# Batch 0 keys sorted for four destinations first, batch 1 values sorted later, column sums on TensorE, and zeros ahead of small products

## The chip, the cores and the metric

One core of a Trainium2 chip. Times are device microseconds (us) of whole executions; profiles are single executions, timed by the hardware profiler from first to last instruction (about 2 us less than the time of a run). The kernel before took 242.44 us (median of 4).

Engines: PE is TensorE (matrix products), PEld its weight loads, DVE VectorE, ACT ScalarE, POOL GpSimd, SP the engine that issues most small DMAs. L12 is line 12 of that run's kernel; line numbers shift by 2 to 28 between the two kernels.

## The reference, cut to what matters

```python
for _ in range(5):                      # P: 4 x 8 matrices of 8 x 8 (Sinkhorn)
    P = exp(P - max(P)); P = P / sum over columns; P = P / sum over rows
k_sorted = einsum('bhij,bhjcd->bhicd', P, k_blocks)      # 8 blocks of 96 tokens
v_sorted = einsum('bhij,bhjcd->bhicd', P, v_blocks)
attn     = softmax(q_block @ k_sorted_block.T / 8) @ v_sorted_block
x = attn as (3072 tokens, 512)
h = x @ w_in                            # 512 -> 2048
out = (s * relu(h)**2 + b) @ w_out      # 2048 -> 512
```

The kernel works on eight tiles of 384 tokens, two per batch. `ffn1(t)` is the first product (its PSUM tile is `hps`) and `ffn2(t)` the second (`ops`). As b is a constant, b times the column sums of w_out is added as a bias.

## The kernel before

All large loads go through one queue, that of POOL, in program order. The values of batches 0 and 2 share the lower half of one tile, those of 1 and 3 the upper half:

```python
vb = const.tile([128, 128, D], BF)
def load_v(rows, prow):
    nc.gpsimd.dma_start(out=vb[prow, 0:BLK, :], in_=vraw[rows])
```

The values of batch 1 are sorted in six pieces (`V1`), written to DRAM and read back in another layout (tile `vs`), as attention needs them with tokens on the partitions:

```python
def v_piece1(c0, eng):                  # two products, one copy, two DMAs to DRAM
    for hf in range(2):
        nc.tensor.matmul(out=ps[hf*64:(hf+1)*64], lhsT=lhsT, rhs=vb[pr, ...], ...)
    evac(vn[:, 0:8, :], ps, eng)
    for hf in range(2): nc.sync.dma_start(out=dv[1][...], in_=vn[...])
```

The schedule around it (cuts marked ...):

```python
warm_up(38); q_half(0, "s"); warm_up(12); build_pd1()
k_piece(0, 0, 16, 1, "v")() ...         # keys of batch 0, all eight destinations
v_piece0(...), s_piece(0, ...) ...      # values and scores of tile 0
q_half(1, "s"); p_piece(0, hp, 0, 2) x4; t_piece(0, "v", 0, 2); s_piece(1, 0); s_piece(1, 1)
load_v(*brows(2))
ffn1(0, Queue([P(0,0,2,2) ... SC(1,3), P(1,0)], 8), 0, 2)
ffn1(0, Queue([V1(0), P(1,1), V1(1), P(1,2), V1(2), P(1,3), V1(3), t_piece(1)], 8), 2, 2)
V1(4)(); V1(5)()
csums(0, 8)                             # on POOL, half of the column sums
v_read(1, nc.sync)                      # values of batch 1 back from DRAM
ffn1(1, Queue([nothing]*4 + [build_pd2] + [nothing]*3, 8))
load_v(*brows(3))
csums(8, NF)                            # on POOL, the other half
# slots of ffn2(0), ffn2(1): q and k pieces of batch 1, then load_k(2), load_k(3), load_q(2),
# S2(2,0) ... P2(2,0) ...               P2(2,0) is the first that needs the values read back
```

`S2` is two score pieces, `P2` two pieces of weighted values, `T` a transposition by DMA. A `Queue` puts its pieces between the products, one per slot.

The softmax here doesn't subtract the row's maximum and nothing guards it: scores larger than these inputs give would overflow.

Of the kernel before, what the change touches and what calls it, by code (L numbers as in the profile page):

```python
# [9 lines left out]
FP = mybir.dt.float32  # L10
# [8 lines left out]
def kernel(  # L19
# [126 lines left out]
            out=w, in_=moe_w_in.rearrange("(hp p) f -> p hp f", p=128)[:, :, c0:c0 + FCH])  # L146
        wis.append(w)
    onesf = const.tile([128, 128], FP)
    nc.gpsimd.memset(onesf, 1.0)

    load_v(*brows(1))
    for f0 in range(0, NF, FW):
# [10 lines left out]
    def wo_at(f):  # L163
        return wos[f // FW][:, f % FW, :]
# [1 line left out]
    jsel = const.tile([128, NB], FP)  # L166
    ks = const.tile([128, 64, BLK], BF)

    def warm_up(n):
        for _ in range(n):  # L170
            wp = psb.tile([128, 256], FP, tag="b", name="wp")
            nc.tensor.matmul(out=wp, lhsT=zt[:, 0:128], rhs=zt, start=True, stop=True)  # L172

    def zero_pad(r0):
# [59 lines left out]
    def q_half(half, eng):  # L234

        if half == 0:
            QT[0] = qtp.tile([128, NHP, S], BF, tag="qt", name="qt0")
        pr = slice(half * 64, half * 64 + 64)
        ps = psa.tile([128, 2, 1024], BF, tag="a", name="tq")
        for hp in range(NHP):  # L240
            for t in range(TQ):
                c0 = (hp % 2) * TG + t * 64
                for e in range(2):
                    nc.tensor.transpose(out=ps[e * 64:(e + 1) * 64, hp // 2, c0:c0 + 64],  # L244
                                        in_=qr[0][pr, 2 * hp + e, t, :], identity=ident[pr, pr])
        for a in range(2):
            evac(QT[0][:, 2 * a:2 * a + 2, half * TG:(half + 1) * TG].rearrange(
                     "q b (p t) -> q b p t", t=TQ),
                 ps[:, a, 0:2 * TG].rearrange("q (b t p) -> q b p t", b=2, t=TQ), eng)
# [15 lines left out]
    def k_piece(b, c0, nc2, nb, eng):  # L265




        pr = brows(b)[1] if nb == 1 else slice(0, 128)  # L270
        rhs = (pd1[pr] if b < 2 else pd2[pr, b - 2]).rearrange("p e m i -> p (e m i)")
        if nc2 * nb > 8:
            ps = psa.tile([128, nc2, nb * 64], FP, tag="a", name="tk")
        else:
            ps = psb.tile([128, nc2, nb * 64], FP, tag="b", name="tk")
        for c in range(nc2):
            nc.tensor.matmul(out=ps[:, c, :],  # L277
                             lhsT=kb[pr, c0 + 2 * c:c0 + 2 * c + 2, :].rearrange("p c d -> p (c d)"),
                             rhs=rhs, start=True, stop=True)
        g0 = (b % 2) * 32  # L280

        def half(cp):
            if b == 0:
                cs = slice(c0 + cp, c0 + 2 * nc2, 2)
            else:
                cs = slice(cp * (BLK // 2) + c0 // 2, cp * (BLK // 2) + c0 // 2 + nc2)
            for e in range(2):
                evac(ks[e * 64:(e + 1) * 64, g0:g0 + nb * 32, cs].rearrange(
                         "p (b g) c -> p b g c", b=nb),
                     ps[cp * 64:(cp + 1) * 64].rearrange(  # L290
                         "p c (b e g) -> p e b g c", b=nb, e=2)[:, e], eng)

        half(0)
        return lambda: half(1)

    def v_piece0(d0, n, eng):

        if n > 8:
            ps = psa.tile([128, n, 64], FP, tag="a", name="tv")
        else:  # L300
            ps = psb.tile([128, n, 64], FP, tag="b", name="tv")
        for t in range(n):
            nc.tensor.matmul(out=ps[:, t, :], lhsT=vb[0:64, :, d0 + t],  # L303
                             rhs=pd1[0:64].rearrange("p e m i -> p (e m i)"),
                             start=True, stop=True)
        evac(VS[0][:, :, d0:d0 + n], ps[0:BLK].rearrange("p t g -> p g t"), eng)
# [42 lines left out]
    def s_piece(t, hp):  # L349

        b, half = divmod(t, 2)
        g0 = (b % 2) * 32 + hp * NB + half * HB
        sc = psa.tile([BLK, 2, 512], FP, tag="a", name="sc")
        for n in range(HB):
            for e in range(2):
                pr = slice(e * 64, (e + 1) * 64)
                q0 = (half * HB + n) * BLK
                nc.tensor.matmul(out=sc[:, e, n * BLK:(n + 1) * BLK], lhsT=ks[pr, g0 + n, :],  # L358
                                 rhs=QT[b][pr, hp, q0:q0 + BLK], start=True, stop=True)
        at = atp.tile([BLK, 2, TG], BF, tag="at", name="at")  # L360
        nc.scalar.activation(out=at, in_=sc[:, :, 0:TG], func=AF.Exp, scale=scale)  # L361
        AT[t, hp] = at

    def p_piece(t, hp, n0=0, nn=HB):

        b, half = divmod(t, 2)
        at = AT[t, hp]
        if t not in X:
            X[t] = xp.tile([BLK, HB, d_model], BF, tag="x", name="x")
        x = X[t]  # L370
        atf = at.rearrange("p e t -> p (e t)")
        if nn < HB:
            p1 = psb.tile([128, 512], FP, tag="b", name="pv")
            pv = [p1[:, e * nn * VW:(e + 1) * nn * VW] for e in range(2)]
            pvv = p1[0:BLK, 0:2 * nn * VW].rearrange("p (e n w) -> p e n w", e=2, w=VW)
        else:
            p2 = psa.tile([128, 2, 512], FP, tag="a", name="pv")
            pv = [p2[:, 0], p2[:, 1]]
            pvv = p2[0:BLK, :, 0:nn * VW].rearrange("p e (n w) -> p e n w", w=VW)
        for e in range(2):  # L380
            for n in range(n0, n0 + nn):
                c0 = (e * HB + n) * BLK
                m = 128 if c0 + 128 <= 2 * TG else BLK
                gi = e * 32 + hp * NB + half * HB + n
                nc.tensor.matmul(out=pv[e][0:m, (n - n0) * VW:(n - n0 + 1) * VW],  # L385
                                 lhsT=atf[:, c0:c0 + m],
                                 rhs=VS[b][:, gi, :], start=True, stop=True)
        rec = rtp.tile([BLK, 2, HB], FP, tag="rec", name="rec")
        nc.vector.reciprocal(out=rec[:, :, 0:nn], in_=pvv[:, :, :, D])  # L389
        nc.vector.tensor_tensor(  # L390
            out=x[:, n0:n0 + nn, hp * 128:(hp + 1) * 128].rearrange("p n (e d) -> p e n d", e=2),
            in0=pvv[:, :, :, 0:D],
            in1=rec[:, :, 0:nn].unsqueeze(3).broadcast_to([BLK, 2, nn, D]), op=ALU.mult)
# [110 lines left out]
    def T(t):  # L504
        return lambda: x_turn(t)

    def attn(t):
        return [S2(t, 0), nothing, P2(t, 0), S2(t, 2), nothing, P2(t, 2), nothing, T(t)]
# [27 lines left out]

    warm_up(38)
    q_half(0, "s")
    warm_up(12)
    build_pd1()  # L540
    k_piece(0, 0, 16, 1, "v")()
    k_piece(0, 32, 16, 1, "s")()
    k_piece(0, 64, 8, 1, "v")()
    k_piece(0, 80, 8, 1, "s")()
    v_piece0(0, 16, "v")
    v_piece0(16, 16, "s")
    v_piece0(32, 16, "v")
    s_piece(0, 0)
    s_piece(0, 1)
    v_piece0(48, 16, "v")  # L550
    s_piece(0, 2)
    s_piece(0, 3)
    q_half(1, "s")
    for hp in range(NHP):
        p_piece(0, hp, 0, 2)
    t_piece(0, "v", 0, 2)
    s_piece(1, 0)
    s_piece(1, 1)

    load_v(*brows(2))  # L560

# [1 line left out]
    def P(t, hp, *r):  # L563
        return lambda: p_piece(t, hp, *r)

    def SC(t, hp):
        return lambda: s_piece(t, hp)

    def V1(i):
        return lambda: v_piece1(i * 8, "v")  # L570

    ffn1(0, Queue([P(0, 0, 2, 2), P(0, 1, 2, 2), P(0, 2, 2, 2), P(0, 3, 2, 2), SC(1, 2),
                   lambda: t_piece(0, "v", 2, 2), SC(1, 3), P(1, 0)], 8), 0, 2)
    ffn1(0, Queue([V1(0), P(1, 1), V1(1), P(1, 2), V1(2), P(1, 3), V1(3),
                   lambda: t_piece(1, "v")], 8), 2, 2)
    V1(4)()
    V1(5)()


    csum = const.tile([128, d_model], FP)  # L580
    gate = sk.tile([1, 1], BF)
    nc.gpsimd.tensor_copy(out=gate, in_=X[1][0:1, HB - 1, d_model - 1:d_model])

    def csums(f0, f1):
        for f in range(f0, f1):
            if f == 1:
                nc.gpsimd.tensor_tensor(out=csum, in0=wo_at(0), in1=wo_at(1), op=ALU.add)
            elif f > 1:
                nc.gpsimd.tensor_tensor(out=csum, in0=csum, in1=wo_at(f), op=ALU.add)  # L589

    csums(0, 8)
    v_read(1, nc.sync)
    ffn1(1, Queue([nothing] * 4 + [build_pd2] + [nothing] * 3, 8))
    load_v(*brows(3))
    csums(8, NF)

    V2 = [lambda c0=c0: v_piece2(c0, "s") for c0 in range(0, BLK, 16)]
    qu = Queue([lambda: q_piece(1, 0, "s"), lambda: q_piece(1, 2, "v")]
# [17 lines left out]
    v_read(2, nc.gpsimd)  # L616
    v_read(3, nc.gpsimd)
    load_q(3)
    at4, at5 = attn(4), attn(5)
    for i, n in enumerate((1, 4, 6)):  # L620
        at4[n] = K(3, 32 * i, 16, "vsv"[i])
    at5[1] = lambda: q_piece(3, 0, "s")
    at5[4] = lambda: q_piece(3, 2, "v")
    qu = Queue(at4 + at5, 24)
    ffn2(2, qu)
    ffn2(3, qu)
    ffn1(4)
# [38 lines left out]
```

## Time and profile before

| stretch of the kernel before | us |
|---|---|
| values of batch 0 landed; first hps | 16.48; 30.59 |
| hps of tile 1; first ops | 50.30; 61.17 |
| last load of values issued; values of batch 1 read back; first used | 57.09; 71.04; 80.27 |
| queries of batch 2 landed; first used | 89.45; 90.94 |
| hps of tile 2; end | 95.75; 241.1 |

(The prediction has 30.66, 61.33 and 80.43 for starts that are 30.59, 61.17 and 80.27 here: it read the chain of waits, which counts a piece from the end of the one before it.)

### The profile page before, as it was taken

What the parts mean: (1) busy time and instruction counts of PE and PEld (TensorE: products, weight loads), DVE (VectorE), ACT (ScalarE), POOL (GpSimd) and SP (SyncE); (2) the same over time, 40 slices, a digit from 0 to 9 for tenths busy, and PEclk for the clock granted to TensorE, in tenths of its full rate; (3) what the DMA queues carried; (4) which work ended last, traced back from release to release, by engine and by line L of the source; (5) the groups of instructions that cost most, each with busy time, mean ns of one, the idle gap of its engine ahead of it and who ended that gap; (6) DMA issues with size and microseconds to landing.
All of it is one profiled execution on the core that took longest, in us unless ns stands there. A gap on an engine that the chain in (4) does not pass through costs nothing.

```text
span 241.1 us, 4882 instructions
## 1 busy us (share of the span) xinstructions
PE 227.1 (94%) x2059; PEld 136.1 (56%) x2080; DVE 134.1 (56%) x268; ACT 107.9 (45%) x154; POOL 39.2 (16%) x52
## 2 busy tenths in 40 slices
PE   8869799989999999999998999999999999999993
PEld 4468698845545555555554455666554556654441
DVE  5775547967993558766465748343353544342221
ACT  6356456435438451677626250656522225660000
POOL 7820000099960000460000000000000000000000
PEclk9965569999999999999999999999999999999998
DMA  4999999985999993599902061400014232001212
GB/s 63 187 199 212 216 201 206 219 206 103 141 153 178 273 307 97 123 120 112 146 7 87 3 152 46 109 0 3 1 52 122 67 111 45 0 3 43 82 48 87
DMA packets 29622, 27.33 MB, mean 113 GB/s; under 512 B 16928, under 2 KB 23840, under 8 KB 29088
## 3 DMA queue, kind: packets, MB, share of 16 engines
q0 software_dynamic: 8400, 15.21, 38.0%
q1 hardware_dynamic: 21200, 11.81, 20.6%
q8 instruction: 16, 0.26, 0.5%
q14 instruction: 6, 0.05, 0.1%
HBM read 29.63 MB, written 8.65 MB: 159 GB/s over the span
## 4 chain that ended last, share of the span: by engine, by line
PE 84%; DVE 6%; DMA 6%; issue 2%; POOL 1%; ACT 1%; POOLq 0%
PE hps L442 34%; PE ops L468 34%; DMA vb<-in_v_dram 6%; PE sc L358 3%; PE pv L385 3%; PE tv L303 2%; PE tk L277 2%; PE tq L259 2%; DVE x L390 2%; PE tv L333 1%; DVE gt L447 1%; DVE vn L228 1%; DVE ot L459 1%; PE tq L244 1%; DVE ks L228 1%
## 5 line engine op out<-in xcount | busy, mean ns | idle before, releaser
L442 PE MATMUL hps<-xt,wi 128*128 128x384 bf16 (+1 forms) x576 | 89.8, 313 | 1.0 <-DVE xt L228 1.0
L468 PE MATMUL ops<-wo,gt 128*128 128x512 bf16 x363 | 87.7, 380 | 1.5 <-issue 0.5
L446 ACT ACTIVATE rt<-hps 128x768 bf16<-128x768 f32 (+1 forms) x72 | 53.2, 739 | 53.7 <-PE hps L442 52.6
L442 PEld LDWEIGHTS <-wi 128*128 128x128 bf16 x576 | 54.6, 100 | 31.3 <-issue 2.3
L447 DVE TENSOR_TENSOR gt<-rt 128x768 bf16<-128x768 bf16 (+1 forms) x72 | 42.0, 585 | 42.2 <-ACT rt L446 41.8
L468 PEld LDWEIGHTS <-gt 128*128 128x128 bf16 x384 | 35.0, 98 | 38.4 <-issue 0.6
L361 ACT ACTIVATE at<-sc 96x768 bf16<-96x768 f32 x32 | 24.3, 802 | 35.2 <-PE sc L358 35.2
L459 DVE SCALAR_TENSOR_TENSOR ot<-ops,s_bc,bias 128x512 f32<-128x512 f32 x24 | 18.0, 749 | 38.0 <-PE ops L468 37.9
L390 DVE TENSOR_TENSOR x<-pv,rec 96x512 bf16<-96x512 f32 (+1 forms) x36 | 22.6, 628 | 1.3
L228 DVE CAST ks<-tk 64x512 bf16<-64x512 f32 (+1 forms) x36 | 20.9, 579 | 4.2 <-PE tk L277 3.8
L589 POOL TENSOR_TENSOR csum<-csum,wo 128x512 f32<-128x512 f32 x14 | 17.6, 1254 | 1.0
L230 ACT CAST ks<-tk 64x256 bf16<-64x256 f32 (+1 forms) x28 | 13.7, 490 | 8.0 <-PE tk L277 7.7
L385 PEld LDWEIGHTS <-at 96*128 96x128 bf16 (+1 forms) x256 | 12.3, 105 | 4.0 <-ACT qt L230 1.0
L385 PE MATMUL pv<-vs,at 96*128 96x66 bf16 (+1 forms) x256 | 13.0, 200 | 0.8 <-DVE rec L389 0.6
L358 PEld LDWEIGHTS <-ks 64*96 64x96 bf16 x256 | 8.4, 132 | 6.8 <-issue 5.0
L389 DVE RECIPROCAL rec<-pv 96x8 f32<-96x8 f32 (+1 forms) x36 | 6.9, 192 | 9.2 <-PE pv L385 9.2
L358 PE MATMUL sc<-qt,ks 64*96 64x96 bf16 x256 | 10.8, 223 | 1.0 <-DVE x L390 1.0
L172 PE MATMUL wp<-zt 128*128 128x256 bf16 x50 | 9.1, 300 | 1.1 <-DVE warm L104 1.1
L277 PEld LDWEIGHTS <-kb 64*128 64x128 bf16 x192 | 6.7, 98 | 5.4 <-issue 5.3
L277 PE MATMUL tk<-pd,kb 64*128 64x64 bf16 x192 | 8.2, 195 | 0.9 <-DVE pd L520 0.9
L230 ACT CAST vn<-tv 128x1024 bf16<-128x1024 f32 x6 | 6.1, 1012 | 4.1 <-PE tv L333 2.3
L303 PE MATMUL tv<-pd,vb 64*128 64x64 bf16 x64 | 6.0, 272 | 1.7 <-DMA vb<-in_v_dram 1.1
(67 smaller groups left out, 101.1 us busy)
## 6 DMA issues: line engine op xcount, KB each, us to landing
out_dram<-ot SPq DMA_DIRECT2D x24, 256.0 KB, 2.2
kb<-in_k_dram POOLq DMA_DIRECT2D x4, 768.0 KB, 10.1
vb<-in_v_dram POOLq DMA_DIRECT2D x4, 768.0 KB, 18.9
qr<-in_q_dram POOLq DMA_DIRECT2D x3, 768.0 KB, 19.3
wi<-in_moe_w_in_dram POOLq DMA_DIRECT2D x2, 1024.0 KB, 18.9
wo<-in_moe_w_out_dram POOLq DMA_DIRECT2D x2, 1024.0 KB, 30.1
dv<-vn SPq DMA_DIRECT2D x6, 256.0 KB, 6.6
vs<-dv POOLq DMA_DIRECT2D x4, 384.0 KB, 11.1
```

Source lines behind the costliest of these rows:

```text
L228: nc.vector.tensor_copy(out=out, in_=in_)
L230: nc.scalar.copy(out=out, in_=in_)
L277: nc.tensor.matmul(out=ps[:, c, :], lhsT=kb[pr, c0 + 2 * c:c0 + 2 * c + 2, :].rearrange("p c d -> p (c d)"), rhs=rhs, start=True, stop=True)
L358: nc.tensor.matmul(out=sc[:, e, n * BLK:(n + 1) * BLK], lhsT=ks[pr, g0 + n, :], rhs=QT[b][pr, hp, q0:q0 + BLK], start=True, stop=True)
L361: nc.scalar.activation(out=at, in_=sc[:, :, 0:TG], func=AF.Exp, scale=scale)
L385: nc.tensor.matmul(out=pv[e][0:m, (n - n0) * VW:(n - n0 + 1) * VW], lhsT=atf[:, c0:c0 + m], rhs=VS[b][:, gi, :], start=True, stop=True)
L390: nc.vector.tensor_tensor(out=x[:, n0:n0 + nn, hp * 128:(hp + 1) * 128].rearrange("p n (e d) -> p e n d", e=2), in0=pvv[:, :, :, 0:D], in1 ...
L442: nc.tensor.matmul(out=hps[:, f, 0:nt], lhsT=wi_at(hp, f0 + f), rhs=xt_at(t, hp, n0, nn), start=(hp == 0), stop=(hp == NHP - 1))
L446: nc.scalar.activation(out=rt[:, :, 0:nt], in_=hps[:, :, 0:nt], func=AF.Relu)
L447: nc.vector.tensor_tensor(out=gt[:, f0:f0 + 2, c0:c0 + nt], in0=rt[:, :, 0:nt], in1=rt[:, :, 0:nt], op=ALU.mult)
L459: nc.vector.scalar_tensor_tensor(out=ot, in0=ops, scalar=s_bc, in1=bias, op0=ALU.mult, op1=ALU.add)
L468: nc.tensor.matmul(out=ops, lhsT=gt[:, f, m * 128:(m + 1) * 128], rhs=wo_at(f), start=(f == 0), stop=(f == NF - 1))
```

## The change

Its intent: let attention of tile 0 start on fewer keys, keep PE's clock up with products of zeros, give POOL's sums to PE (four column tiles side by side), spread the pieces more evenly (the six value pieces of batch 1 move from hps of tile 0 to hps of tile 1), and reorder one late queue. The diff, cut to its core:

```diff
-    warm_up(12)
+    warm_up(20)
     build_pd1()
-    k_piece(0, 0, 16, 1, "v")() ... k_piece(0, 80, 8, 1, "s")()
+    warm_up(9)
+    k_half(0, 24, 0, "v")               # keys for destinations 0 to 3 only
+    k_half(48, 24, 0, "s")
 ...
-    q_half(1, "s")
-    for hp in range(NHP):
-        p_piece(0, hp, 0, 2)
+    k_half(0, 16, HB, "s", psa)         # destinations 4 to 7
+    p_piece(0, 0, 0, 2, 2)              # two zero products ahead of each
+    p_piece(0, 1, 0, 2, 2)
+    k_half(32, 16, HB, "s", psa)
+    p_piece(0, 2, 0, 2, 2); p_piece(0, 3, 0, 2, 2)
     t_piece(0, "v", 0, 2)
-    s_piece(1, 0); s_piece(1, 1)
+    warm_up(2, psa)
 ...
+    ffn1(0, Queue([P x4, t_piece, k_half(64, 16, HB, "s"), q_half(1, "s"), SC(1, 0)], 8), 0, 2)
+    ffn1(0, Queue([SC(1, 1), SC(1, 2), SC(1, 3), P(1, 0) ... P(1, 3), t_piece(1)], 8), 2, 2)
-    V1(4)(); V1(5)(); csums(0, 8) on POOL; v_read(1, nc.sync)
-    ffn1(1, Queue([nothing] * 4 + [build_pd2] + [nothing] * 3, 8))
+    csums()                              # 16 products on PE, out[32 g] += ones * w_out[f]
+    ffn1(1, Queue([V1(i) for i in range(6)] + [lambda: v_read(1, nc.sync), build_pd2], 8))
     load_v(*brows(3))
-    csums(8, NF) on POOL
 ...                                      # third ops: two of three key copies to ACT,
                                          # empty slots behind the scores
```

More of the change, by code (lines that the diff above doesn't have):

```diff
@@ L148 @@
     onesf = const.tile([128, 128], FP)
-    nc.gpsimd.memset(onesf, 1.0)
+    nc.gpsimd.memset(onesf, 1.0 / 32)
+    ones = const.tile([128, 32], BF)
+    nc.gpsimd.memset(ones, 1.0)
     load_v(*brows(1))
@@ L167, with warm_up @@
     ks = const.tile([128, 64, BLK], BF)
-    def warm_up(n):
+    def warm_up(n, pool=psb):
+        wp = pool.tile([128, 256], FP, tag="b" if pool is psb else "a", name="wp")
         for _ in range(n):
-            wp = psb.tile([128, 256], FP, tag="b", name="wp")
             nc.tensor.matmul(out=wp, lhsT=zt[:, 0:128], rhs=zt, start=True, stop=True)
@@ L294, in k_piece, with k_half @@
         return lambda: half(1)
+    def k_half(c0, nc2, i0, eng, pool=psb):
+        pr = slice(0, 64)
+        h = 1 if nc2 * 32 <= 512 else 2
+        if h == 1:
+            ps = pool.tile([128, 1, 512], FP, tag="b" if pool is psb else "a", name="tk")
+        else:
+            ps = psa.tile([128, 2, 512], FP, tag="a", name="tk")
+        rhs = pd1[pr].rearrange("p e m i -> p (e m) i")[:, :, i0:i0 + HB]
+        n = nc2 // h
+        for c in range(nc2):
+            nc.tensor.matmul(out=ps[:, c // n, c % n * 32:(c % n + 1) * 32],
+                             lhsT=kb[pr, c0 + 2 * c:c0 + 2 * c + 2, :].rearrange("p c d -> p (c d)"),
+                             rhs=rhs, start=True, stop=True)
+        for b in range(h):
+            for cp in range(2):
+                for e in range(2):
+                    c1 = c0 + 2 * n * b + cp
+                    evac(ks[e * 64:(e + 1) * 64, 0:32, c1:c1 + 2 * n - 1:2].rearrange(
+                             "p (m i) c -> p m i c", i=NB)[:, :, i0:i0 + HB, :],
+                         ps[cp * 64:(cp + 1) * 64, b, 0:n * 32].rearrange(
+                             "p (c e m i) -> p e m i c", e=2, m=NHP, i=HB)[:, e], eng)
     def v_piece0(d0, n, eng):
@@ L362, in s_piece, with p_piece @@
         AT[t, hp] = at
-    def p_piece(t, hp, n0=0, nn=HB):
+    def p_piece(t, hp, n0=0, nn=HB, zeros=0):
         b, half = divmod(t, 2)
@@ L374, in p_piece @@
             pv = [p1[:, e * nn * VW:(e + 1) * nn * VW] for e in range(2)]
+            for _ in range(zeros):
+                nc.tensor.matmul(out=p1[:, 272:512], lhsT=zt[:, 0:128], rhs=zt[:, 0:240],
+                                 start=True, stop=True)
             pvv = p1[0:BLK, 0:2 * nn * VW].rearrange("p (e n w) -> p e n w", e=2, w=VW)
@@ L538 @@
     q_half(0, "s")
-    warm_up(12)
+    warm_up(20)
     build_pd1()
-    k_piece(0, 0, 16, 1, "v")()
-    k_piece(0, 32, 16, 1, "s")()
-    k_piece(0, 64, 8, 1, "v")()
-    k_piece(0, 80, 8, 1, "s")()
+    warm_up(9)
+    k_half(0, 24, 0, "v")
+    k_half(48, 24, 0, "s")
     v_piece0(0, 16, "v")
     v_piece0(16, 16, "s")
+    s_piece(0, 0)
     v_piece0(32, 16, "v")
-    s_piece(0, 0)
     s_piece(0, 1)
-    v_piece0(48, 16, "v")
+    v_piece0(48, 8, "v")
+    v_piece0(56, 8, "s")
     s_piece(0, 2)
     s_piece(0, 3)
-    q_half(1, "s")
-    for hp in range(NHP):
-        p_piece(0, hp, 0, 2)
+    k_half(0, 16, HB, "s", psa)
+    p_piece(0, 0, 0, 2, 2)
+    p_piece(0, 1, 0, 2, 2)
+    k_half(32, 16, HB, "s", psa)
+    p_piece(0, 2, 0, 2, 2)
+    p_piece(0, 3, 0, 2, 2)
     t_piece(0, "v", 0, 2)
-    s_piece(1, 0)
-    s_piece(1, 1)
+    warm_up(2, psa)
     load_v(*brows(2))
@@ L570, in V1, with csums @@
         return lambda: v_piece1(i * 8, "v")
-    ffn1(0, Queue([P(0, 0, 2, 2), P(0, 1, 2, 2), P(0, 2, 2, 2), P(0, 3, 2, 2), SC(1, 2),
-                   lambda: t_piece(0, "v", 2, 2), SC(1, 3), P(1, 0)], 8), 0, 2)
-    ffn1(0, Queue([V1(0), P(1, 1), V1(1), P(1, 2), V1(2), P(1, 3), V1(3),
-                   lambda: t_piece(1, "v")], 8), 2, 2)
-    V1(4)()
-    V1(5)()
-    csum = const.tile([128, d_model], FP)
-    gate = sk.tile([1, 1], BF)
-    nc.gpsimd.tensor_copy(out=gate, in_=X[1][0:1, HB - 1, d_model - 1:d_model])
-    def csums(f0, f1):
-        for f in range(f0, f1):
-            if f == 1:
-                nc.gpsimd.tensor_tensor(out=csum, in0=wo_at(0), in1=wo_at(1), op=ALU.add)
-            elif f > 1:
-                nc.gpsimd.tensor_tensor(out=csum, in0=csum, in1=wo_at(f), op=ALU.add)
-    csums(0, 8)
-    v_read(1, nc.sync)
-    ffn1(1, Queue([nothing] * 4 + [build_pd2] + [nothing] * 3, 8))
+    def csums():
+        cs = psb.tile([128, d_model], FP, tag="b", name="cs")
+        for f in range(NF):
+            g = f % 4
+            nc.tensor.matmul(out=cs[g * 32:(g + 1) * 32], lhsT=ones[:, 0:32], rhs=wo_at(f),
+                             start=(f < 4), stop=(f >= NF - 4))
+        nc.scalar.copy(out=csum, in_=cs)
+    ffn1(0, Queue([P(0, 0, 2, 2), P(0, 1, 2, 2), P(0, 2, 2, 2), P(0, 3, 2, 2),
+                   lambda: t_piece(0, "v", 2, 2), lambda: k_half(64, 16, HB, "s"),
+                   lambda: q_half(1, "s"), SC(1, 0)], 8), 0, 2)
+    csum = const.tile([128, d_model], FP)
+    ffn1(0, Queue([SC(1, 1), SC(1, 2), SC(1, 3), P(1, 0), P(1, 1), P(1, 2), P(1, 3),
+                   lambda: t_piece(1, "v")], 8), 2, 2)
+    csums()
+    ffn1(1, Queue([V1(i) for i in range(6)] + [lambda: v_read(1, nc.sync), build_pd2], 8))
     load_v(*brows(3))
-    csums(8, NF)
     V2 = [lambda c0=c0: v_piece2(c0, "s") for c0 in range(0, BLK, 16)]
@@ L618 @@
     load_q(3)
-    at4, at5 = attn(4), attn(5)
-    for i, n in enumerate((1, 4, 6)):
-        at4[n] = K(3, 32 * i, 16, "vsv"[i])
-    at5[1] = lambda: q_piece(3, 0, "s")
-    at5[4] = lambda: q_piece(3, 2, "v")
-    qu = Queue(at4 + at5, 24)
+    qu = Queue([S2(4, 0), K(3, 0, 16, "s"), nothing, P2(4, 0), nothing, S2(4, 2), nothing,
+                K(3, 32, 16, "s"), P2(4, 2), nothing, T(4), K(3, 64, 16, "v"), S2(5, 0), nothing,
+                lambda: q_piece(3, 0, "s"), P2(5, 0), nothing, S2(5, 2), nothing,
+                lambda: q_piece(3, 2, "v"), P2(5, 2), T(5), nothing, nothing], 24)
     ffn2(2, qu)
```

## The prediction

> **What bounds the kernel now.** I read the engine table and the slices first, then stretches of 3.41 us (the step in which the clock record changes), then the chain of waits.
>
> ```profile
> PE 227.1 (94%) x2059; PEld 136.1 (56%) x2080; DVE 134.1 (56%) x268; ACT 107.9 (45%) x154; POOL 39.2 (16%) x52
> ...
> PE   8869799989999999999998999999999999999993
> ...
> PEclk9965569999999999999999999999999999999998
> ```
>
> The matrix engine (PE) is the bound over the whole span, so a change can only pay where PE waits or runs at a low clock. That is slices 3 to 6, and two short gaps.
>
> ```profile
> 10.99:14.40 3.41, 1.37 (x35) 1.29 (x35) 1.83 (x9) 0.94 (x2) 1.04 (x2) 1.00 1.01 212
> 14.40:17.81 3.41, 2.27 (x37) 2.13 (x32) 3.33 (x6) 3.09 (x5) 0.54 (x1) 0.50 1.16 195
> 17.81:21.23 3.42, 3.42 (x48) 3.42 (x48) 2.55 (x5) 2.68 (x5) 0.00 (x0) 0.50 1.12 212
> ...
> 28.06:31.47 3.41, 3.06 (x38) 2.40 (x36) 1.86 (x6) 1.27 (x3) 0.00 (x0) 0.50 0.98 183
> 31.47:34.88 3.41, 3.41 (x28) 3.19 (x27) 1.58 (x6) 1.39 (x3) 0.00 (x0) 0.50 1.23 206
> 34.88:40.00 5.12, 5.12 (x82) 4.67 (x81) 3.25 (x11) 3.77 (x8) 0.00 (x0) 1.00 1.24 206
> 40.00:50.30 10.30, 9.26 (x119) 7.24 (x116) 9.73 (x23) 4.26 (x9) 2.40 (x3) 1.00 1.19 216
> ...
> 123.10:127.95 4.85, 3.83 (x45) 2.09 (x45) 4.64 (x9) 0.81 (x1) 0.00 (x0) 1.00 0.09 31
> ```
>
> Columns: stretch, length, busy us of PE, PEld, DVE, ACT, POOL, clock, DMA share, GB/s. PE works only 1.37 of 3.41 us before 14.40; then the clock is halved for 20.5 us, six steps, until the first step full of wide products ends (34.88). From 40 to 50 VectorE (DVE) is busy 9.73 of 10.30 us: it, not PE, sets the pace there. In 123 to 128 PE lacks 1.0 us.
>
> ```profile
> 2.68 13.80 DMA vb<-in_v_dram
> 16.48 0.14 issue
> 16.62 4.38 PE tv L303 x47
> ...
> 28.97 0.88 PE tr L413 x8
> 29.85 0.80 PE sc L358 x10
> 30.66 0.43 PE hps L442 x2
> ```
>
> The chain shows that the values of batch 0 land at 16.48 whatever the engines do; from there the first feed-forward product (hps) starts at 30.66. hps of the second tile starts at 50.30 and ops, the second product, at 61.33, after which PE is dense (33.86 of 34.49 us to 95.82). So the question is: when does ops start in the changed kernel?
>
> **What the Trainium skill says.** "TensorE: Matmul & The Clock Gate", Part 1 (The HAM clock gate), says that idleness halves the clock and a busy window of about 3.4 us restores it. The trace agrees: steps of 3.41 us, 1.00 to 0.50 and back. It names no share of activity that suffices; the trace says that 1.37 of 3.41 us drops it and that 3.06 of 3.41 us of mostly narrow work does not restore it. "TensorEngine Tiling (Array Packing)", Theoretical Speedup, gives up to 4 times for a small dimension of 32 or less. Two 64-column products of the value sort, side by side (tv L319), took 0.33 us on the chain for 2 x 0.21 us of streaming, starting 3 ns apart, so columns do run side by side here. "SBUF — State Buffer", Who interferes with whom, says a VectorE instruction with two SBUF inputs contends with GpSimd reads. gt took 0.56 us in quiet stretches and up to 0.80 us beside the sums on POOL, but PE was dense there, so ending that buys nothing.
>
> **The change part by part.**
>
> 1. Zeros: 12 become 20 before the build of pd1, 9 follow it. A zero product starts every 0.16 us at full clock (12 in 9.03 to 10.9), so 20 end near 12.2, when pe starts, and 9 run from 12.6 to 14.0. PE busy in the step 10.99 to 14.40 rises from 1.37 to about 3 us, so I expect no drop at 14.40. The next step stays doubtful: key products of 32 columns at about 29 ns each (the rate of 64 columns at full clock) end near 15.4, then PE idles to 16.6, so about 2.1 of 3.41 us are busy, with half the rows and little streaming.
>
> 2. Keys sorted for half the destinations first: an eviction carries 192 elements instead of 512 or 256. These took 0.755 and 0.45 us start to start, so 192 cost about 0.36, and eight per engine 2.9 instead of 4.9 us. DVE is free at 17.5 instead of 19.1, ACT at 18.2 instead of 19.5. The other half comes back as three times four evictions of 256 elements, all on ACT: 3 x 1.9 = 5.6 us, and 48 more products, 1.4 us of PE.
>
> 3. From 16.6 to the first hps with a full clock: 64 value products (spaced 90 ns at half clock; 40 to 90 now, as the strided weight load may limit them), 16 score products per piece 0.4 us, half P pieces 0.15 plus two zeros 0.2, the two key pieces 0.5 each, t 0.5. Walking buffers and engines in order, ACT does one value eviction (1.0), four exponentials (0.71 to 0.8), a half value eviction (0.6) and two key pieces (3.7), and is free at 26.3 to 29. First hps at about 27.3 (26 to 28.5), 3.4 us earlier than 30.66.
>
> 4. But what was done before 30.66 moves behind it: the second q half (0.8 of PE, 1.4 of ACT), two score pieces, the third key piece. hps of tile 0 is 16 steps of 8 products of 0.0825 = 0.66 us: 10.6. Add eight P pieces (2.2), two t pieces (1.3), four score pieces (1.6), q (0.8), key piece (0.5): 17.0 us of PE. It will not be dense. ACT from the key piece to the fourth exponential has 1.85 + 1.4 + 4 x 0.71 + 5 x 0.41 = 8.1 us, where PE has six steps and these pieces, 6.4: 1.7 lost. Then four P pieces lie back to back: DVE 0.30 (gt) + 0.13 + 0.69 = 1.12 per step against PE 0.96: 0.6 lost. Waits for q, t and x add about 1. Sum 20.3 us, to 47.6.
>
> 5. csums: 16 products of 512 columns in four column tiles. Done singly 16 x 0.216 = 3.5 us; four side by side 0.9, say 1.3. It fills the wait for xt (1.0 us before). hps of tile 1 starts at about 49, 1.3 us earlier than 50.30.
>
> 6. Six value pieces now sit in hps of tile 1, which is PE bound: 6 x 0.33 = 2.0 us more there; 10.4 + 0.36 (pe) + 2.0 = 12.8. ops starts at 61.8: **0.5 us later** than before.
>
> 7. The reordered queue in the third ops: two key evictions go from DVE to ACT with empty slots behind scores. The 1.0 us lost from 123 to 128 should go.
>
> Sum at full clock: +0.5 - 1.0 = -0.5 us of 242.7. The gain of the clock (about 2 us of the 4.2 us of hps at half rate, and denser values) is eaten by the added products and by what moves behind it.
>
> **The rivals.** (a) The clock falls at 17.81 instead of 14.40. For: the step to 17.81 streams little, as the one that dropped before did (by my count 0.3 of its time in both). Against: PE is busy 0.6, not 0.4, of the step, and the zeros in the P pieces look tuned. Then values, scores and extra zeros run at half rate: first hps near 32, full clock near 31.5 to 35, ops about 5 us later than before, total 245 to 248. I give this a third. (b) The ACT and DVE binding of step 4 is milder, because evictions of different banks overlap and value weights load in 30 ns: first hps at 25.5, hps of tile 1 near 46.5, total 239. For: DVE and ACT together have room in 16 to 50. Against: [...]the waits are in the order itself. (c) csums wait for w_out, which landed at 42.44 before; with csums near 47.6 this is hidden, and single-file columns would add 2.2 us. (d) The value round trip of batch 1 through DRAM starts later and delays P of tile 2. Its last copy landed at 71.04 before and was first used at 80.43; a shift of some 5 us still fits.
>
> **Range and chances.** Full clock, two thirds: 242.2, with 2 us either way. Half clock, a third: about 246. That both kernels come from a line of tuning speaks for the lower side, so I take 242.0, with 238.0 to 247.0. Faster by over 2% needs below 237.8, so ops 4 us earlier than before, which no sum above gives: 0.11. Slower by over 2% needs above 247.5: 0.12. Within 2%: 0.77.
>
> **What would show it.** Slices 3 to 6 of the clock row read 9 if the clock holds; a 5 after 17.8 makes rival (a). The first hps should stand at 26 to 28.5; one at 32 refutes step 3. ACT should be the releaser of PE in the end of the first pass of hps and DVE in the second half of the other (step 4); if PE is dense there, (b) holds. The sixteen cs products should take 1 to 1.5 us; 3.5 refutes side by side. ops should start within 1.5 us of 61.3, and 123 to 128 lose under 0.3 us. A clock that holds together with an ops start before 58 would make the prediction wrong, and so would a new wait for values in tile 2.

## More of the kernel before

The timeline of POOL (start, length, what) shows in what order the loads went out:

```profile
47.82 0.24 POOL L582 COPY gate<-x 1x1 bf16<-1x1 bf16 x1 [23.08 <-DVE x L390]
48.02 1.14 POOL L587 TENSOR_TENSOR csum<-wo 128x512 f32<-128x512 bf16 x1
49.24 7.91 POOL L589 TENSOR_TENSOR csum<-csum,wo 128x512 f32<-128x512 f32 x6
57.09 0.54 POOL L91 DMA_DIRECT2D vb<-in_v_dram  x1
57.65 10.59 POOL L589 TENSOR_TENSOR csum<-csum,wo 128x512 f32<-128x512 f32 x8
68.18 0.54 POOL L88 DMA_DIRECT2D kb<-in_k_dram  x1
```

The last load of values stands between the two halves of the sums; keys follow.

Just before that load the DMA engines are little used (stretch, length, busy us of PE, PEld, DVE, ACT, POOL, clock, DMA share, GB/s), and the two reads that bring the values of batch 1 back take 9.6 and 11.9 us:

```profile
53.00:57.00 4.00, 4.00 (x26) 2.26 (x24) 2.38 (x4) 2.43 (x3) 3.84 (x3) 1.00 0.28 79
...
DMA to landing us min/median/max: 9.6/10.7/11.9
```

## The result

The changed kernel took 254.31 us (median of 4, 253.56 to 256.29) against 242.44: **5.1% slower**, ratio 1.051 with a 95% interval of 1.044 to 1.058. Ratios here are the mean time of one kernel's fast runs over that of the other's of the same rounds, so not quite the ratio of the medians. Executions over 1.5% slower than the fastest of the same kernel are left out of the means. The output was correct.

The page of the changed kernel, in the lines that answer to those of before (busy time by engine; then PE and its clock in 40 slices):

```profile
PE 234.4 (92%) x2151; PEld 141.1 (56%) x2171; DVE 124.1 (49%) x264; ACT 114.2 (45%) x172; POOL 20.4 (8%) x37
...
PE   8679998899999649999999999999999999999993
...
PEclk9965579999999958999999999999999999999999
```

Slices 14 and 15 of the PE row are new: a 6 and a 4, in a part that was dense before, and the clock row shows a 5 and an 8 just behind. The half clock in slices 3 to 6 is still there. Stretches of the changed kernel (length, busy us of PE, PEld, DVE, ACT, POOL, clock, DMA share, GB/s):

```profile
38.00:47.00 9.00, 7.96 (x158) 6.71 (x156) 2.34 (x7) 8.62 (x17) 0.00 (x0) 1.00 1.26 214
47.00:53.76 6.76, 5.73 (x89) 4.70 (x88) 5.78 (x14) 2.25 (x6) 0.00 (x0) 1.00 0.70 147
...
54.40:64.50 10.10, 10.10 (x60) 4.64 (x58) 5.80 (x10) 4.60 (x6) 0.00 (x0) 1.00 0.23 50
64.50:76.80 12.30, 11.93 (x137) 6.85 (x138) 8.71 (x15) 5.64 (x8) 2.08 (x4) 1.00 0.77 152
76.80:86.50 9.70, 9.50 (x69) 4.22 (x67) 4.46 (x7) 6.85 (x8) 0.37 (x1) 1.00 1.20 186
86.50:92.40 5.90, 0.03 (x2) 0.01 (x1) 0.00 (x0) 0.21 (x1) 0.00 (x0) 0.79 1.33 186
...
93.35:96.76 3.41, 3.41 (x12) 1.21 (x11) 1.46 (x3) 0.65 (x1) 0.00 (x0) 0.50 0.72 273
```

From 86.5 to 92.4 hardly any engine works, and the DMA engines are full; from 54.4 to 64.5 it is the other way round: PE is full and the DMA engines move 50 GB/s, for 10 us where it was 4 before. Work that could have been moved early is moved late. The chain of waits (start, length, what) says what PE stood for; below it, how long the two reads took:

```profile
65.36 0.61 DVE vn L230
65.97 0.02 issue
65.98 0.45 SPq L350
66.43 0.04 issue
66.47 10.29 DMA dv<-vn
...
77.29 15.06 DMA vs<-dv
92.35 0.05 issue
92.40 1.11 PE pv L413 x16
...
DMA to landing us min/median/max: 12.9/14.0/15.1
```

The last value piece goes to DRAM in 10.29 us and comes back in 15.06 us; before, its write took 2.07 us (56.59 to 58.66) and the trip back at most 11.9 us. POOL's timeline shows why the traffic starts late:

```profile
64.55 0.52 POOL L91 DMA_DIRECT2D vb<-in_v_dram  x1 [39.72 <-PE tv L344]
65.06 0.52 POOL L88 DMA_DIRECT2D kb<-in_k_dram  x1
75.75 0.52 POOL L88 DMA_DIRECT2D kb<-in_k_dram  x1 [10.17 <-PE tk L279]
76.26 0.91 POOL L81 DMA_DIRECT2D qr<-in_q_dram  x1
```

POOL stood 39.72 us in front of the last load of values, until PE had read the old values (tv L344, the six value pieces). It went out at 64.55 instead of 57.09, and everything behind it in the queue went with it.

Where the 13.1 us between the two profiles (254.2 and 241.1) lie, by marks on PE:

| from, to | before | changed | difference |
|---|---|---|---|
| start to hps of tile 1 | 50.30 | 53.76 | +3.5 |
| hps of tile 1 to first ops | 10.87 | 13.49 | +2.6 |
| first ops to hps of tile 2 | 34.58 | 42.72 | +8.1 |
| hps of tile 2 to the end | 145.4 | 144.2 | -1.1 |

The profiled execution is the slowest of the four; the others spanned 251.5 to 252.7 us. Part of the +3.5 belongs to it: in e1 and e5 below, whose PE has the same pieces in the same order up to there, hps of tile 1 starts at 52.21 and 51.41.

### The profile page after: what moved, and what is told of

Same layout as the page of the kernel before. It is cut to its first block, busy times and chain, and to the rows that moved or that the text cites. A ratio compares the mean times of both kernels' runs of the same rounds, so it can differ in the third digit from the quotient of the medians.

```text
span 254.2 us, 5064 instructions
## 1 busy us (share of the span) xinstructions
PE 234.4 (92%) x2151; PEld 141.1 (56%) x2171; DVE 124.1 (49%) x264; ACT 114.2 (45%) x172; POOL 20.4 (8%) x37
## 4 chain that ended last, share of the span: by engine, by line
PE 74%; DMA 11%; ACT 6%; DVE 5%; issue 2%; SPq 0%
PE hps L470 31%; PE ops L496 29%; DMA vs<-dv 6%; DMA dv<-vn 4%; PE pv L413 3%; PE sc L383 3%; ACT rt L474 2%; ACT ks L232 2%; PE tv L328 2%; PE tk L279 1%; ACT at L386 1%; PE tq L261 1%; PE tk L309 1%; DMA sn<-in_sort_net_dram 1%; DVE gt L475 1%
## 5 line engine op out<-in xcount | busy, mean ns | idle before, releaser
L470 PE MATMUL hps<-xt,wi 128*128 128x384 bf16 (+1 forms) x576 | 90.9, 314 | 1.7 <-ACT rt L474 0.9
L496 PE MATMUL ops<-wo,gt 128*128 128x512 bf16 x364 | 88.7, 384 | 1.6 <-issue 0.6
L475 DVE TENSOR_TENSOR gt<-rt 128x768 bf16<-128x768 bf16 (+1 forms) x72 | 36.9, 513 | 51.9 <-ACT rt L474 51.4
L232 ACT CAST ks<-tk 64x256 bf16<-64x256 f32 (+2 forms) x44 | 19.7, 447 | 8.3 <-PE tk L279 4.7
L413 PEld LDWEIGHTS <-at 96*128 96x128 bf16 (+1 forms) x256 | 13.4, 109 | 9.4 <-DMA vs<-dv 6.4
L230 DVE CAST ks<-tk 64x512 bf16<-64x512 f32 (+2 forms) x32 | 16.3, 509 | 1.6 <-PE tk L309 1.0
L174 PE MATMUL wp<-zt 128*128 128x256 bf16 x69 | 10.1, 312 | 1.1 <-DVE warm L104 1.1
L174 PEld LDWEIGHTS <-zt 128*128 128x128 bf16 x69 | 7.4, 111 | 2.8 <-DVE warm L104 1.1
L230 DVE COPY qt<-tq 128x1536 bf16<-128x1536 bf16 x4 | 7.0, 1758 | 2.7 <-PE tq L261 2.7
L279 PEld LDWEIGHTS <-kb 64*128 64x128 bf16 x144 | 4.8, 95 | 4.4 <-issue 4.4
```

What stands on the lines that cost most here:

```text
L174: nc.tensor.matmul(out=wp, lhsT=zt[:, 0:128], rhs=zt, start=True, stop=True)
L230: nc.vector.tensor_copy(out=out, in_=in_)
L232: nc.scalar.copy(out=out, in_=in_)
L413: nc.tensor.matmul(out=pv[e][0:m, (n - n0) * VW:(n - n0 + 1) * VW], lhsT=atf[:, c0:c0 + m], rhs=VS[b][:, gi, :], start=True, stop=True)
L470: nc.tensor.matmul(out=hps[:, f, 0:nt], lhsT=wi_at(hp, f0 + f), rhs=xt_at(t, hp, n0, nn), start=(hp == 0), stop=(hp == NHP - 1))
L475: nc.vector.tensor_tensor(out=gt[:, f0:f0 + 2, c0:c0 + nt], in0=rt[:, :, 0:nt], in1=rt[:, :, 0:nt], op=ALU.mult)
```

## The experiments

Twelve kernels ran; all were correct. Theories: **R**, the round trip is slow because the loads, no longer held back by sums on POOL, stand ahead of it; **D**, formed after the first four, that the held load of values leaves the DMA engines idle and makes everything behind it late; **S**, that ops starts late because ACT and DVE bind in the first tile's hps. The kernel before ran beside each group of four: 242.9, 242.04 and 242.74 us.

| run | us | ratio to before | 95% |
|---|---|---|---|
| e1_gate | 255.94 | 1.0545 | 1.0505 to 1.0586 |
| e2_poolsums | 257.22 | 1.0544 | 1.047 to 1.0618 |
| e3_valuesback | 246.11 | 1.0163 | 1.011 to 1.0216 |
| e4_zeros | 255.16 | 1.0497 | 1.0452 to 1.0541 |
| e5_ownvalues | 245.76 | 1.0154 | 1.0117 to 1.019 |
| e6_dve | 246.96 | 1.0200 | 1.0148 to 1.0253 |
| e7_queue | 241.26 | 0.9955 | 0.9915 to 0.9994 |
| e8_nozeros | 247.13 | 1.0192 | 1.0147 to 1.0238 |
| e9_split | 246.04 | 1.0145 | 1.0123 to 1.0168 |
| e10_valuesmoved | 249.22 | 1.0247 | 1.0202 to 1.0293 |
| e11_best | 242.96 | 1.0016 | 0.9997 to 1.0035 |
| e12_bestzeros | 243.7 | 1.0040 | 1.0018 to 1.0061 |

**e1_gate: the later loads wait for the values.** On the changed kernel:

```diff
-    [seq(lambda: load_k(*brows(2)), ...
+    def gate1(): nc.gpsimd.tensor_copy(out=gt1, in_=VS[1][:, 0, 0:1])
+    [seq(gate1, lambda: load_k(*brows(2)), ...
```

> The changed kernel with one small POOL copy more: it reads the first column of the values of batch 1 as they came back from DRAM, and stands before the key and query loads of batches 2 and 3, so those loads wait until the values have landed. Theory R (the 5.9 us stall of PE at 86.5 to 92.4 is the value round trip, slowed because the loads, no longer held back by the sums on POOL, stand ahead of it in the DMA queues): the last value copy lands at 78 to 82 instead of 92.35, no stall, no half clock after it, 245 to 248 us, ops still starting near 67. Rival (the round trip is late only because the value pieces come later in the program): it lands after 86 and the time falls by less than 2 us.

A miss that taught most. The values landed at 81.5 us as expected and their wait was gone, but the time was 255.94 us: the stall stood elsewhere. Who waited, longest first, from 80 to 110 us:

```profile
PEld L261 <- DMA qr<-in_q_dram: 8.5, 1, 8.5
PE tq L261 <- DMA qr<-in_q_dram: 8.0, 1, 8.0
```

PE now stood 8.0 us for the queries of batch 2, which landed at 103.5. Competition is real, but this gate only chose who is late. The rival, that position alone counts, falls too: the values came early by order alone.

**e2_poolsums: the sums back on POOL.**

```diff
-    csums()                              # 16 products on PE
+    nc.gpsimd.tensor_copy(out=gate, in_=X[1][...]); csums(0, 8)      # on POOL
     load_v(*brows(3))
+    csums(8, NF)                         # on POOL
```

> The changed kernel with the column sums of w_out back on POOL, half of them ahead of the second tile's hps and half behind the load of the last values, as in the kernel before. Theory R: the sums hold the key load of batch 2 back to about 75 us by accident, the values land near 80 to 82, the stall of 5.9 us goes: 246 to 248 us. Rival (position of the value pieces alone): the values still land near 90, 253 to 255 us. A third view, that the column products on PE cost time themselves (16 x 0.216 = 3.5 us): the second tile's hps would start 2 us earlier; I expect under 0.5 us, as xt is waited for anyway.

Theory R missed: the sums did hold the key load back, to 76.72 (65.06 in the changed kernel), yet a gap of 5.68 us stayed (87.9 to 93.5), the second half of the values landing at 93.5. The last load of values was still issued at 65.82, as its wait for the value pieces was still there. The sums on POOL had not been the guard.

**e3_valuesback: the value pieces back in the first hps.**

```diff
-    ffn1(0, Queue([SC(1,1), SC(1,2), SC(1,3), P(1,0), ...], 8), 2, 2); csums()
-    ffn1(1, Queue([V1(i) for i in range(6)] + [v_read, build_pd2], 8))
+    ffn1(0, Queue([SC(1,1), V1(0), SC(1,2), V1(1), ... V1(5), P(1,3), t_piece(1)], 8), 2, 2); csums()
+    v_read(1, nc.sync)
+    ffn1(1, Queue([nothing] * 4 + [build_pd2] + [nothing] * 3, 8))
```

> The changed kernel with the six value pieces of batch 1 back in the second half of the first tile's hps, between the score and P pieces, and the read back issued ahead of the second tile's hps; the sums stay on PE. Theory R and its rival both expect the stall gone (values land near 70 to 75). Theory S (ops starts 5.9 us late because the first hps binds on ACT and DVE, and because 6 value pieces make the second hps 2.5 us longer): the second hps takes 11.0 instead of 13.5 us, the first gets 0 to 1.5 us longer as the value pieces fill waits of PE, ops starts at 65 to 66, in all 244 to 246.5 us. If PE were dense in the first hps, ops would start at 67 as before and the time be near 247.

The stall went: values back at 73.9, 246.11 us. The second hps took 10.86 us, the first got longer, and ops started at 65.15, within what was expected. So the place of the value pieces decides the stall, but both the round trip and the load behind it had moved.

**e4_zeros: more zeros, to hold the clock.**

```diff
-    warm_up(20)
+    warm_up(36)
     k_half(48, 24, 0, "s")
+    warm_up(8)
```

> The changed kernel with 36 zero products instead of 20 ahead of pe and 8 more between the key and the value products, as the trace showed that 20 end at 11.1 us and pe starts at 12.9. View 1: the clock stays whole past 14.84, the first hps starts at 27 to 28 instead of 30.15, and all later work moves up by 3 to 5 us: 249 to 251.5 us. View 2: the thin value products (half the rows, 64 columns) drop the clock one step later, at about 18.25, and the time stays at 253 to 255.

View 2, its 253 to 255 us just missed. The clock held to 18.21 instead of 14.84, then fell although PE was busy 3.37 of 3.41 us by the record:

```profile
14.80:18.21 3.41, 3.37 (x58) 3.02 (x54) 3.00 (x9) 2.48 (x7) 0.54 (x1) 1.00 1.21 206
```

That the added zeros moved the fall is not shown: with the early zeros of the changed kernel it came at 14.48 in e3 and at 19.28 in e1, as the steps of 3.41 us lie differently in each execution. Nor did it matter: the first hps started at 29.36 in e3, 29.33 in e1 and 29.94 here, and the time was within the noise of the changed kernel's. One more thing shows here: the value products started every 92 ns at full clock (16.5 to 18.2) and every 89 ns at half clock. Their pace is not the array's clock, so holding it there gains nothing. The key products, as short, started every 25 ns in this run.

**e5_ownvalues: another tile for the values of batches 2 and 3.** This takes away what the load waits for:

```diff
+    vb2 = const.tile([128, BLK, D], BF)
 def load_v(rows, prow):
-    nc.gpsimd.dma_start(out=vb[prow, 0:BLK, :], ...)
+    dst = vb if rows.start < 128 else vb2
+    nc.gpsimd.dma_start(out=dst[prow, 0:BLK, :], ...)       # v_piece2 reads vb2
```

> The changed kernel with a tile of their own for the values of batches 2 and 3, so that their loads need not wait until the value products of batches 0 and 1 have read the old tile. The first four runs refuted the sums on POOL as the gate (with them back the stall stayed) and showed that holding key and query loads back only moves the stall to the queries. Theory D: the DMA queues stood nearly idle from 54 to 64.5 us because the load of the last values waits for the value pieces that the change moved, and all that follows in the queue is late by 7.5 us, whatever its order. Then here the loads fill that time, the values are read back by 78, no stall of PE over 1 us, ops still starts at 65 to 67: 245 to 247.5 us. Rival (the traffic after 64 us is too much in itself, or the value pieces alone are too late): a stall of over 3 us stays, 250 to 254 us.

Theory D holds: 245.76 us, some 8.5 us below the changed kernel, with every other part of the change in place. In POOL's timeline the loads of values go out at 18.51 and 23.44, the keys of batch 2 at 36.70:

```profile
18.51 0.53 POOL L93 DMA_DIRECT2D vb<-in_v_dram  x1 [1.33 <-DMA qr<-in_q_dram]
23.44 0.52 POOL L93 DMA_DIRECT2D vb<-in_v_dram  x1 [4.39 <-DMA wi<-in_moe_w_in_dram]
36.70 0.52 POOL L89 DMA_DIRECT2D kb<-in_k_dram  x1 [12.75 <-PE tk L311]
```

and the same stretches as shown of the changed kernel read:

```profile
54.40:64.50 10.10, 10.10 (x60) 4.82 (x58) 6.62 (x12) 4.87 (x6) 0.00 (x0) 1.00 0.70 158
64.50:76.80 12.30, 12.26 (x147) 6.61 (x147) 9.47 (x17) 4.94 (x7) 1.42 (x2) 1.00 1.10 104
76.80:86.50 9.70, 9.70 (x74) 4.74 (x73) 3.92 (x7) 7.14 (x9) 0.00 (x0) 1.00 1.09 227
86.50:92.40 5.90, 5.90 (x69) 3.38 (x68) 2.55 (x6) 3.08 (x4) 0.00 (x0) 1.00 0.78 280
...
DMA to landing us min/median/max: 6.3/7.6/8.8
```

158 GB/s where the changed kernel moved 50, PE full where it stood, and the two reads of the values back (last line) in 6.3 and 8.8 us. The last value piece stands as near to ops as in the changed kernel (its last write is issued 0.7 us ahead of the first ops, there 0.8), so the place of the pieces alone costs no stall.

**e6_dve: key and query copies to VectorE**, on e3:

```diff
-    k_half(64, 16, HB, "s"), q_half(1, "s")
+    k_half(64, 16, HB, "v"), q_half(1, "v")
```

> The run with the value pieces back, with one edit more: the third key piece and the second half of the queries are copied out by VectorE instead of ScalarE. Theory S (in the second half of the first tile's hps PE waits for ScalarE, which was busy 8.6 of 9 us from 38 to 47): the second tile's hps starts 1 to 2 us earlier than in that run, 244.2 to 245.3 us. Rival (PE and VectorE bind there, as the value pieces share VectorE with P): no gain, within 0.5 us of 246.1.

A miss: 246.96 us, no gain; ACT fell from 7.85 to 5.81 busy us in 38 to 47, DVE rose from 4.29 to 6.64, and PE stayed at 7.8 to 8.0. The profiled execution is the slowest of the four, and its clock fell once more (53.70 to 57.11).

**e7_queue: the kernel before with the reordered third ops alone.**

```diff
-    qu = Queue(attn(4) + attn(5) with K at 1, 4, 6 ("vsv"), 24)
+    qu = Queue([S2(4, 0), K(3, 0, 16, "s"), nothing, P2(4, 0), nothing, ...], 24)
```

> The kernel before with nothing of the change but the reordered queue of the third ops (two of three key evictions on ScalarE, empty slots behind scores). Prediction step 7: the 1.0 us that PE lost from 123 to 128 goes, nothing else moves: 0.9 to 1.3 us below the kernel before, 241.2 to 242.0. If the loss only moves to a later piece, under 0.3 us.

241.26 against 242.04 us, an interval just below 1. The stretch in which PE lacked a microsecond is full:

```profile
123.10:127.95 4.85, 4.85 (x51) 2.60 (x50) 2.35 (x5) 2.77 (x5) 0.00 (x0) 1.00 0.16 57
```

This is the one part of the change that is shown to pay (the halved keys did not run alone), and the best kernel: 0.45% below the kernel before and over 5% below the changed one.

**e8_nozeros: no zeros ahead of P and of the first hps**, on e3:

```diff
-    p_piece(0, 0, 0, 2, 2) ... warm_up(2, psa)
+    p_piece(0, 0, 0, 2) ...
```

> The run with the value pieces back, without the two zero products ahead of each of the four half P pieces and without the two ahead of the first hps (the early zeros stay). The zeros took about 0.4 us a pair at half clock: the first hps starts 1 to 1.7 us earlier. View 1: the zeros only cost, the clock comes back at the same step, time 1 to 1.5 us lower, 244.6 to 245.2. View 2: the zeros bring the full clock back a step (3.4 us) earlier; without them it returns later, so 1 us is given back: 245.8 to 247.

The first hps started 1.6 us earlier than in e3 (27.77 against 29.36), and the time was 247.13 us: as much was given back. The second tile's hps started no earlier (54.41 against 54.29), and in this profile the clock fell once more, from 53.07 to 56.48. The intervals of e3 and e8 overlap; what the zeros are worth is under the noise.

**e9_split: the third key copy on VectorE, the queries on ScalarE**, on e5:

```diff
-    k_half(64, 16, HB, "s"), q_half(1, "s")
+    k_half(64, 16, HB, "v"), q_half(1, "s")
```

> The run with the values' own tile, with the third key piece copied out by VectorE and the query half still by ScalarE, so that the two copies, 1.84 and 1.5 us one after the other on one engine in every run so far, lie side by side. Theory S, mended (moving both to VectorE gained nothing because they still stood in a row): the first score piece behind them starts 1 to 1.8 us earlier and the second tile's hps 0.7 to 1.8 us earlier, 244.0 to 245.1 us. Rival (the binding only passes on to VectorE behind P): within 0.4 us of 245.8.

The PE gap of 0.71 us ahead of the first score piece was gone, but the second tile's hps started at 51.56 against 51.41, and the time is that of e5. The profiled execution got its full clock back 1.6 us later (33.06 against 31.43), which may hide a gain of under a microsecond. Theory S in its simple form, one engine to relieve, is not borne out.

**e10_valuesmoved: the kernel before with the value pieces moved, nothing else.**

```diff
-    ffn1(0, Queue([V1(0), P(1,1), V1(1), P(1,2), V1(2), P(1,3), V1(3), t_piece(1)], 8), 2, 2)
-    V1(4)(); V1(5)(); csums(0, 8); v_read(1, nc.sync)
-    ffn1(1, Queue([nothing] * 4 + [build_pd2] + [nothing] * 3, 8))
+    ffn1(0, Queue([P(1,1), P(1,2), P(1,3), t_piece(1)], 8), 2, 2); csums(0, 8)
+    ffn1(1, Queue([V1(i) for i in range(6)] + [v_read, build_pd2], 8))
```

> The kernel before with one edit of the change alone: the six value pieces of batch 1, and with them the read back and the load of the last values, move from the first tile's hps to the second's. Theory D: the second hps takes 13.4 instead of 11.0 us, the first ends 1 to 2.5 us earlier as VectorE bound it; the load of the last values is issued 3 to 6 us later, the values are read back after 84 us, PE waits 2 to 7 us for them: 245 to 250 us. Rival (the stall needs the rest of the change too): no wait of PE over 1 us for the values, 242 to 244 us.

249.22 us (247.25 to 253.43): one edit makes half of the loss, with the sums still on POOL. The load of values went out 3 us later (60.02), and PE stood 3.02 us, though not for the values (back at 79.95) but for the queries, which landed at 95.64 instead of 89.45; they had 1.5 us of slack before. The clock halved for 3.4 us behind it. The expectation had the right size and the wrong victim.

**e11_best and e12_bestzeros: tries at a better version**, on e7:

```diff
 e11: + vb2 as in e5; csums() on PE behind V1(4), V1(5), in place of POOL's
 e12: e11 with warm_up(30), warm_up(8), one buffer per warm_up, and two zeros ahead of the first four half P pieces of tile 0
```

> A try at a version that beats both: the kernel before with the reordered queue, the column sums on PE in four column tiles, and the values' own tile. The sums (1.05 us) fit into the wait for xt of 1.05 us, the tile keeps the freed loads off the value round trip: 240.3 to 241.3 us. If the sums push the second hps back, or the loads now ahead of the read back delay it: 241.5 to 244.

> The same with the zeros of the change: 30 and 8 early ones and two ahead of each of the first four half P pieces. In the run with 36 zeros PE was busy 3.37 of 3.41 us from 14.8 to 18.2 and the clock fell all the same, so narrow products do not hold it. View 1: the zeros ahead of P bring the clock back a step (3.4 us) earlier and save 0.5 to 1.5 us: 239.3 to 240.6. View 2: they cost 1.6 us ahead of the first hps and save as much: within 0.5 us of the run without.

Neither beats e7. In e11 the sums are not free: behind two value pieces they wait for a PSUM buffer that VectorE must empty first, and hps of tile 1 starts at 51.62 instead of 50.30. In the changed kernel no value piece stands there, and the sums fit. The zeros of e12 gained nothing.

## Why the prediction was wrong

**The step that failed is rival (d)**, "a shift of some 5 us still fits". It looked at one transfer (back at 71.04, used at 80.43) and moved it as if the others stood still. The values came back 21.3 us later, not 5: the last write was issued 9.9 us later (66.47 instead of 56.59), took 8.2 us longer, and the read back 3.2 us longer. The value pieces hold a load, and that load holds the queue: four loads, the write and the read back then share the DMA engines from 64.5 on, having been nearly idle for 10 us. The read back took up to 15.1 us instead of at most 11.9, and landed at 92.35 instead of the 76 that the prediction allowed. That is 5.87 us of standing still, and by my estimate 2.2 us more because the clock halved from 89.93 to 96.76 (4.4 us of products at half rate). It is the "new wait for values in tile 2" that the prediction named as a sign of being wrong. e5 shows the cause by removing the hold alone, e10 makes a stall in the old kernel with one edit, though one that moves the round trip too, and e1 and e2 show what does not help. The sum of the prediction has 0 in this place; 8.1 is what it measured. The sum is 13.6 us too low in all: 8.1 here, 4.8 up to hps of tile 1, 0.7 in step 6. Without the stall the kernel stands at 245.76 (e5), where the prediction put the half clock, to which it gave a third.

**Step 1, zeros.** Mis-sized and then beside the point. The rate of 0.16 us came from products that each took a new buffer; with one buffer, 20 took 2.2 us, ended at 11.1, and pe started at 12.94 as the sort matrix had landed 0.65 us later. The clock fell at 14.84, in the step in which it fell before (14.40). More zeros did not keep it (e4). Rival (a) had the half clock right, though a step later.

**Step 3, first hps at 27.3.** It came at 30.15, 0.4 us ahead of the kernel before. The value products were allowed 40 to 90 ns; e4 measured 92 even at full clock, so the hope that a full clock would speed the values had no ground.

**Steps 4 and 5.** From the first hps to that of tile 1 the prediction has 21.7 us and the profile 23.6, with 5.2 us of it at half clock. ACT set the pace there as foretold, busy 8.62 of 9 us from 38 to 47, but e6 and e9 show that relieving it alone gains nothing. Each P step took 1.40 us and not 1.12: in the chain hps (0.83) and rt (0.50) follow each other, so the latencies add instead of the busiest engine setting the pace. The sums took 1.05 us for 16 products, within the 1 to 1.5 foretold: four starting 3 to 4 ns apart, then the next four 0.22 us later.

**Step 6.** 12.8 foretold, 13.49 measured: a value piece cost 0.43 us and not 0.33 in that place (eight products take 1.74 us with one and 1.31 without). Together steps 1 to 6 put ops at 67.25 instead of 61.8; in e5 it is 64.9; that execution got its clock back at 31.43 instead of 35.32. These steps are what is left in e5 and e3: about 1.5% over the kernel before.

**Step 7** was right: 1.0 us foretold, 1.1 measured, alone in e7 too.

**One reading was too low.** Beside the sums on POOL gt took up to 1.51 us in the kernel before, not 0.80 (0.56 in the changed kernel, where the sums are on PE). In e2 and e10 the sums run beside the value pieces: gt took up to 1.91 us, and the last value copy started 2.8 us behind the start of its products instead of 1.4. So both runs hold this delay besides what they test.

The smaller terms stand by and large; the result was decided by a queue that the prediction treated as slack. What stays open: why the first hps, with PE, ACT and DVE each less than full, is not shortened by moving a copy; what share of it the half clock has, as the clock's steps fall differently in each execution; and which of the early edits, the halved keys among them, makes the 1.5% that is left.

## What to carry to other kernels

When you move work that reads a buffer, look up which load waits for that read, and then everything that stands behind this load in the same queue: the slack of the first transfer is not the slack of the last. Idle DMA engines a few microseconds ahead of a stretch in which they are full are the sign in the profile, and here a buffer of its own for the held load took the stall away with the pieces left in place (e5). Putting the pieces back did as well (e3: 246.11 us against 245.76), and in the kernel before, which had no stall, the buffer gained nothing (e11). Zeros that keep a unit busy gained nothing here, where something else set the pace.

## What the Trainium skill lacked or had wrong

- "TensorE: Matmul & The Clock Gate", Part 1 (The HAM clock gate), speaks of busy and idle windows. It lacks what counts as busy: with PE busy 3.37 of 3.41 us in products of 64 rows, 32 or 64 columns, with a few zeros between, the clock fell (e4); with 2.36 of 3.41 us, mostly of wide products, it held (kernel before, 48.54 to 51.95), and with 2.01 of 3.41 it fell (e6, 50.29 to 53.70). So a window need not be idle to end in half clock, and the busy time of the record does not tell which does.
- The same page, LDWEIGHTS (loading the stationary operand), reckons a load from its number of columns alone, by its formula an estimate of 128 / 1.2 = 107 ns here; its next section, Weight-path perf modes, has a faster load for 128 columns of bf16, "packed or strided", and no cost of the stride. Products with packed weights of 128 columns started every 25 ns (keys, 32 columns streamed, e4) or 29 ns (keys, 64 columns, kernel before); with weights whose columns lie 128 bytes apart, every 89 to 93 ns at either clock (values, 64 columns). No run changes the layout alone, so that it is the cause is not shown.
- "Trainium Kernel Development and Optimization", Key Constraints, says that DMAs from all issuing engines run on the same 16 DMA engines and interleave. This case agrees, and adds the size: the same read back of values took 6.3 to 8.8 us from issue to landing with most loads out of the way (e5) and 12.9 to 15.1 us among them (changed kernel), and a 64 KB write of values 1.9 us alone (issued at 57.28) and 10.3 us behind two loads (at 66.47).
